# Taps of one block as diagonal matmuls, two vector subtractions fewer, and a new instruction order, in a two-branch sequence kernel

## The chip, the cores and the metric

The kernel runs on one core of a Trainium2 chip. A core has a matrix engine (TensorE, PE in the profile, with its weight loads listed as PEld), a vector engine (VectorE, DVE), an activation engine (ScalarE, ACT), GpSimd (POOL) and SyncE (SP), which here only issues DMAs. The engines run side by side, each through its own instruction list in order, and wait for each other by semaphores. The metric is the device time of one execution in microseconds (us); lower is better.

## The reference

Two independent branches over 2048 positions of 576 channels are computed and set side by side in the output. Branch A is attention with 32 heads of 18 channels, in which each position looks at itself and seven earlier ones, two apart. Branch B gates a long convolution. Its first step, the shift with four taps, is what the change touches.

```python
# A: dilated local attention
q, k, v = split(x @ wqkv)                       # 32 heads of 18
logits  = einsum("bhsd,bhswd->bhsw", q, kg) * scale      # kg: k at s, s-2, ..., s-14
a       = einsum("bhsw,bhswd->bhsd", softmax(logits), vg) @ wo
# B: shift, long convolution, gate
for t in range(4):
    k_shift = k_shift + k_pad[:, t:t + S, :] * shift_k[:, 3 - t]
kv = k_shift * v
y  = irfft(rfft(kv, 2S) * rfft(ssm_k, 2S))[:S] + kv * ssm_D
b  = q * y
out = concatenate([a, b], axis=-1)
```

## The kernel before, in words

**Order.** All work is cut into named jobs, and the string `ORDER` lists the names. The last loop of the kernel calls them in that order, and each engine gets its instructions in the order of the calls; nothing reorders them afterwards. A setup of fixed order goes ahead of the list: loads of x, weights, k and v, index tables and masks on POOL, the tables of sines, the first projections. A quotation mark behind a projection's or output's name means that its short tail matmuls go first instead of last. PSUM is handed out in four slots of two banks each (`banks`, `slots`): a job that finds none free waits for the engine that empties the oldest.

**Branch A.** `q`, `k`, `v` jobs (`project`, line 317) multiply 128x128 weight blocks by 512 columns of x, with tails of 64 rows, and a fifth column tile of 64. `L` jobs (line 701) are the products of queries with shifted keys on DVE; `G` jobs (line 712) sum them over a head's channels on PE with 32 weight columns. `sm` jobs are the softmax, `D` jobs spread its weights by DMA on SP's queue, `V` jobs (line 808) multiply by the values on DVE, `A` jobs (line 816) sum over the eight positions on PE with 64x64 identities, `O` jobs (line 871) are the output projection.

**Branch B.** The sequence is cut into four blocks of 512 positions. `Lk`, `Lv` load a block of k and v. `T0` to `T3` (`taps`, line 511) do the four taps and the product with v. For this k lies seven rows deep in each partition (`kj`), so that a shift is another row; DVE multiplies two rows at a time by the spread taps `skb`, adds the halves into a pair of buffers, and multiplies by v. The result is `kv`. `M` jobs (line 538) fold a block into sums and differences of its two halves, with the matrix `fold` as weights, since position pairs lie in neighbouring partitions. `x` jobs (line 677) transform it to frequencies. `Lf` jobs load the filter by transposing DMAs on SP's queue, `Fr` corrects first rows (six small DMAs on SP's queue, one on POOL's), `F` jobs (line 592) fold the filter and `K` jobs (line 612) transform it. `Lw` loads the weights of v, and `RG` jobs regroup them on ACT. 

For each output block j, third t of the channels and earlier block i, `p` jobs (line 948) multiply spectra on DVE and `z` jobs (line 960) add the products up in PSUM with 64x64 identities on PE. Block 3 takes four products per third. For the thirds named in `JOINED` (line 42), a `y` job (line 957) first subtracts the third product from the first on DVE, and the `z` job of the third product falls away. `i`, `b` and `g` jobs transform back, mirror and multiply by the gate; the stores go out from there.

**Memory.** `Ks` holds 12 parts of 2304 columns. The setup uses the middle and the end for x and for tables; the first parts stay empty until the transformed filters of blocks 3 and 2 are written there by K jobs. `xw` holds x, its weights and the four blocks of kv (`KVS`).

Of the kernel before, what the change touches and what calls it, by code (L numbers as in the profile page):

```python
# [12 lines left out]
ALU = mybir.AluOpType  # L13
FP32 = mybir.dt.float32
BF16 = mybir.dt.bfloat16
# [2 lines left out]
PSUM = bass.MemoryType.PSUM  # L18

ORDER = """  # L20
    T0 k03a' T1 S1 k03b I1 k02a k02b Lk2 Lv2 I0 k00a' Lk3 Lv3 M01 X5 k00b q10a Ex q10b Lf3 T2 Lo3 q13a' q13b
    k10a k10b T3 k13a' Lf2 k13b q12a q12b N2 Lo2 k01a M10 k01b Lf1 M00 k11a k11b q11a M11 q11b Lf0 N3 Lw SV L001
    k12a M20 k12b x001 M21 x021 q24a x020 q24b x000 Lo1 k24a Fr Lo0 Z2 N1 RG3 k24b RG2 F3 RG0 F2 L000 K310 G000
    K311 K210 K211 L002 K313 G001 RG4 F1 G002 L003 G003 K302 L004 G004 K301 L010 K212 L011 K303 K213 K203 N0 F0
    L012 K200 K300 G010 L013 K201 K312 K202 RG1 G011 G012 K113 K103 G013 L014 G014 K112 K102 K101 L100 K100 K010
    K111 K110 sm0a K001 K013 sm0b v24a' L101 v24b L102 G100 L103 G101 K012 sm0c sm0d U3 U2 K000 K011 K003 G102
    K002 D0 D1 v11a v11b G103 L104 G104 ak00 M30 v12a' v12b ak02 v01a ak01 L110 G110 M31 L111 G111 v01b v00a'
    L112 G112 L113 Wl v00b G113 x031 U1 L114 G114 V04 v10a' v10b A04 sm1a sm1b v02a v02b v03a' sm1c v03b x201
    V10 V11 sm1d V12 A10 v13a' v13b D2 x330 x310 x301 V13 A11 V20 V21 x200 x331 x230 x010 x221 A20 x321 V22 x210
    x011 V23 D3 V34 ax02 x220 x030 x300 D4 A21 V40 V41 A34 D5 O000' x211 V42 x320 x231 x111 x131 Tx2 A40 V43  # L30
    x120 x101 ax00 x130 ax01 V50 x121 x311 O001 A41 V51 O100' p000 x100 x110 O010 A50 V52 z000 O011' V53 O101
    A51 Tk2 p010 z010 ax10 O020' O021 p020 z020 O110' ak10 i000 p200 i02880 Q0 p100 z100 p101 p110 p111 Q1 z101
    i02881 i001 p121 p120 O111 z110 p201 z111 z120 p210 z121 O120 p211 z200 z210 z211 p212 z212 z201 p202 z202
    Tx3 p220 Tk3 p221 O030' p222 O121 b0288 z220 p301 z221 O031' p302 b00 z222 p303 i200 i100 g0 Q2 p300 y300
    p312 i12880 i201 i101 i12881 z300 z301 z303 p310 p311 y310 O130 b10 b1288 p313 g1 Q3 p322 O131' z310 p320
    z311 p321 z313 i22880 i300 b20 y320 p323 i22881 i301 b2288 g2 z320 z321 z323 b30 i3384L g30 g3384
"""

LHOMES = (0, 1, 2, 0, 1, 2, 0, 1, 2, 0, 1, 2, 0, 1, 0, 1, 0, 1, 0, 1)
VHOMES = (0, 1, 2, 0, 1, 2, 0, 1, 2, 0, 1, 2, 0, 1, 2, 0, 1, 2)  # L40
OHOMES = (0, 1, 1, 0, 2, 0, 1, 0)
JOINED = ("300 310 320").split()
PHOMES = (0, 1, 2, 3, 0, 1, 2, 3, 0, 4, 1, 2, 3, 0, 4, 1, 2, 3, 0, 1, 2, 3, 0, 1, 2, 3, 0, 1, 2, 3)


def view(t, offset, dims):

    return bass.AP(tensor=t.tensor, offset=t.offset + offset, ap=[list(t.ap[0])] + [list(d) for d in dims])
# [3 lines left out]
def kernel(  # L52
# [13 lines left out]
    nc = tc.nc  # L66
    Bsz, S, D = A_x.shape
# [6 lines left out]
    kf = B_k.flatten_outer_dims()  # L74
    vf = B_v.flatten_outer_dims()
# [45 lines left out]
    def kv_of(i):  # L121
        return view(xw, HB * KVS[i], [[D, 4], [1, D]])
# [26 lines left out]
    tB = sp1.tile([128, 8 * D], BF16, name="tB")  # L149
    skrow = tB[0:97, 0:4 * D]  # L150
    nc.scalar.dma_start(skrow[96:97, :], B_shift_k.rearrange("d j -> (d j)").unsqueeze(0))
    warm = main.tile([128, 1], FP32, name="warm")
    nc.scalar.activation(warm[:], pib[:], ACT.Sin)
    ones96 = sp1.tile([97, 256], BF16, name="ones96")
# [19 lines left out]

    def kTok(m):
        return view(Ks, k_at(m, 2), [[D, 4], [1, D]])
    kjs, vts = [], []
# [6 lines left out]
    def load_k(i):  # L184

        eng = nc.sync
        kj = sp1.tile([128, 7, D], BF16, name="kj", bufs=2)
        r0 = BL * i
        low = [(0, 64)]
        if i == 0:  # L190
            nc.gpsimd.memset(kj[0:1, 0:3, :], 0.0)
            nc.gpsimd.dma_start(kj[0:1, 3:7, :], kf[0:4, :].unsqueeze(0))
            low = [(1, 49), (49, 64)]
        for a, b in ((3, 7), (0, 3)) if i == 0 else ((0, 7),):
            for p0, p1 in low:
# [5 lines left out]
        kjs.append(kj)  # L201

    def load_v(i):
        vt = sp1.tile([128, 4, D], BF16, name="vt", bufs=2)
        nc.sync.dma_start(vt[0:128:2], vf[BL * i:BL * i + 256, :].rearrange("(p c) d -> p c d", c=4))
        nc.sync.dma_start(vt[1:128:2], bass.AP(tensor=vf.tensor, offset=vf.offset + (BL * i + 256 + 3) * D,
                                              ap=[[4 * D, 64], [-D, 4], [1, D]]))
        vts.append(vt)

    def load_filter(m):  # L210

# [49 lines left out]
    for h in range(2):  # L261
        f = fold[:, 64 * h:64 * h + 64]
        nc.gpsimd.affine_select(f, ones128[:, 0:64], pattern=[[-2, 64]], compare_op=ALU.is_equal, fill=0.0,
                                base=0, channel_multiplier=1)
        nc.gpsimd.affine_select(f, f, pattern=[[2, 64]], compare_op=ALU.not_equal, fill=(1.0, -1.0)[h],
                                base=-127, channel_multiplier=1)
    flip2 = main.tile([128, 128], BF16, name="flip2")
    nc.gpsimd.tensor_scalar(flip2[:], flip[:], 2.0, None, op0=ALU.mult)
    ident2 = main.tile([128, 128], BF16, name="ident2")
# [215 lines left out]
    for n in range(2):  # L485
        project_first(1, 2 * n)
        sines[3 - 3 * n]()
    def job(name, fn, *args):

        assert name not in jobs  # L490
        jobs[name] = partial(fn, *args)
# [19 lines left out]
    def taps(i):  # L511
# [23 lines left out]
            add(pair[1])  # L535
        tt(kv, kv, vt, ALU.mult)
# [599 lines left out]
```

## Time and profile before

| | |
|---|---|
| median of 3 runs | 206.83 us (206.75 to 206.92) |
| profiled execution, first to last instruction | 204.6 us |
| instructions | 5004, of them 2074 matmuls |
| largest group on PE, projections of L322 | 38.5 us, 160 matmuls |
| pair products on DVE (L706) | 31.7 us, 16 instructions |
| spectral products on DVE (L950) | 9.5 + 18.9 + 9.5 + 2.7 us by place of the result |
| tap multiplications on DVE (L517) | 19.3 us, 8 instructions |
| evictions of filter units on ACT (L618) | 18.6 us, 32 instructions |
| moved by DMA | 38.48 MB, mean 188 GB/s |

The profiled execution's own time isn't listed apart from its span. The median of the three runs is 2.2 us longer than the span, which leaves out what lies ahead of the first instruction and behind the last.

How to read the profile: a row of a group gives line, engine, operation, tile written and tiles read, shapes and count, then busy time and mean duration, then the idle time of the engine just before it and what ended that. The chain that ended last is followed back from the last instruction, at each step to what released it or to the instruction before it on its engine. A piece of the chain has a start, a length and a count. Matmuls are pipelined, so the duration of one (380 ns for 512 columns) is longer than the distance from one to the next, and a share of busy time alone doesn't prove that PE is full.

### The profile page before, as it was taken

How to read it: one execution, taken by the hardware profiler on the slowest of the kernel's cores; microseconds unless marked ns; L12 is line 12 of the kernel's file. 1: busy time of each engine (PE TensorE's matmuls, PEld its weight loads, DVE VectorE, ACT ScalarE, POOL GpSimd, SP SyncE). 2: the span in 40 equal slices, each digit the busy share in tenths (PEclk: the TensorE clock that was granted, in tenths of full speed). 3: DMA queues.
4: the chain of work that ended last, by engine and by line, in shares of the span. 5: the costliest groups of instructions: out<-in, count | busy, mean ns of one | idle time of the engine just before them, and what ended most of it. 6: DMA issues, size and time to landing. Idle time of an engine off the chain costs nothing.

```text
span 204.6 us, 5004 instructions
## 1 busy us (share of the span) xinstructions
PE 196.9 (96%) x2074; PEld 109.9 (54%) x2074; DVE 192.3 (94%) x146; ACT 155.6 (76%) x223; POOL 60.8 (30%) x106
## 2 busy tenths in 40 slices
PE   7999999999989999999999999999999999999990
PEld 2543544334455646543245556776666767766660
DVE  7559999999999999999999999999999999899992
ACT  4788995678899999966578678886778767767760
POOL 8989500011348581400380000004090001030300
PEclk9999999999999999999999999999999999999997
DMA  6999899989509869999899990879989303944555
GB/s 197 280 293 306 175 289 373 214 177 281 169 3 146 111 82 185 167 180 222 157 235 216 248 244 34 141 183 334 186 227 233 100 28 122 227 130 145 153 182 150
DMA packets 34916, 38.48 MB, mean 188 GB/s; under 512 B 17523, under 2 KB 28911, under 8 KB 34894
## 3 DMA queue, kind: packets, MB, share of 16 engines
q1 hardware_dynamic: 26668, 24.29, 46.5%
q0 software_dynamic: 5760, 11.36, 29.5%
q10 hardware_dynamic: 2466, 2.51, 3.6%
q8 instruction: 16, 0.26, 0.5%
q14 instruction: 6, 0.05, 0.1%
HBM read 13.11 MB, written 4.72 MB: 87 GB/s over the span
## 4 chain that ended last, share of the span: by engine, by line
PE 88%; DMA 3%; ACT 2%; DVE 2%; issue 1%; SPq 1%; DVEq 0%
PE ps_proj L322 18%; PE ps_fx L682 8%; PE ps_wo L888 8%; PE ps_z L975 8%; PE ps_inv L1010 7%; PE ps_acc L824 7%; PE ps_fk L567 5%; PE ps_log L720 5%; DMA Ks<-in_A_x_dram 3%; PE ps_proj L333 3%; PE ps_proj L326 3%; PE ps_proj L439 3%; PE ps_fk L568 3%; PE ps_fold L545 2%; PE ps_wo L880 1%
## 5 line engine op out<-in xcount | busy, mean ns | idle before, releaser
L322 PE MATMUL ps_proj<-xw 128*128 128x512 bf16 x160 | 38.5, 380 | 0.0
L706 DVE TENSOR_TENSOR av<-qk 128x4096 bf16<-128x4096 bf16 (+1 forms) x16 | 31.7, 2014 | 0.1
L322 PEld LDWEIGHTS <-xw 128*128 128x128 bf16 x160 | 13.9, 98 | 19.4 <-issue 5.7
L988 ACT ACTIVATE av<-ps_z 128x768 bf16<-128x768 f32 x23 | 17.2, 811 | 6.5 <-PE ps_z L975 6.0
L517 DVE TENSOR_TENSOR tB<-kj,skb 128x4608 bf16<-128x4608 bf16 (+1 forms) x8 | 19.3, 2416 | 0.1
L950 DVE TENSOR_TENSOR qk<-xw,Ks 128x2304 bf16<-128x2304 bf16 x14 | 18.9, 1354 | 0.3 <-PE ps_z L975 0.3
L684 ACT ACTIVATE xw<-ps_fx 128x576 bf16<-128x576 f32 x32 | 18.6, 665 | 0.3 <-PE ps_fx L682 0.2
L618 ACT ACTIVATE Ks<-ps_fk 128x576 bf16<-128x576 f32 x32 | 18.6, 699 | 0.2 <-PE ps_fk L568 0.2
L355 ACT ACTIVATE qk<-ps_proj 128x1024 bf16<-128x1024 f32 x14 | 14.3, 1023 | 5.2 <-PE ps_proj L333 2.8
L888 PE MATMUL ps_wo<-qk 128*128 128x288 bf16 x128 | 17.9, 287 | 0.0
L626 POOL DMA_DIRECT2D Ks<-Ks x8 | 10.1, 1426 | 26.0 <-PE ps_back L1059 19.3
L682 PE MATMUL ps_fx<-xw,TB 128*128 128x288 bf16 x128 | 17.7, 287 | 0.0
L567 PE MATMUL ps_fk<-Ks,TB 128*128 128x384 bf16 x62 | 16.5, 327 | 0.1
L824 PE MATMUL ps_acc<-av,ident 64*64 64x512 bf16 x160 | 15.3, 378 | 0.0
L1010 PE MATMUL ps_inv<-av,TI 128*128 128x288 bf16 (+1 forms) x112 | 15.2, 292 | 0.0
L568 PE MATMUL ps_fk<-Ks,TB 128*128 128x192 bf16 x62 | 15.2, 246 | 0.0
L682 PEld LDWEIGHTS <-TB 128*128 128x128 bf16 x128 | 11.9, 98 | 5.9 <-issue 2.7
L888 PEld LDWEIGHTS <-qk 128*128 128x128 bf16 x128 | 11.7, 98 | 5.4 <-issue 2.7
L355 ACT ACTIVATE v<-ps_proj 128x1024 bf16<-128x1024 f32 x9 | 9.3, 1033 | 6.5 <-PE ps_proj L322 4.5
L813 DVE TENSOR_TENSOR av<-Ks,v 128x4096 bf16<-128x4096 bf16 x6 | 13.5, 2286 | 0.0
L827 ACT ACTIVATE qk<-ps_acc 128x1024 bf16<-128x1024 f32 x8 | 8.2, 1024 | 6.7 <-PE ps_acc L824 6.7
L1010 PEld LDWEIGHTS <-TI 128*128 128x128 bf16 x112 | 10.6, 98 | 4.2 <-issue 1.1
(195 smaller groups left out, 441.6 us busy)
## 6 DMA issues: line engine op xcount, KB each, us to landing
Ks<-Ks POOLq DMA_DIRECT2D x8, 576.0 KB, 7.8
TB<-av SPq DMA_DIRECT2D x12, 256.0 KB, 5.4
kj<-in_B_k_dram SPq DMA_DIRECT2D x6, 504.0 KB, 7.0
vt<-in_B_v_dram SPq DMA_DIRECT2D x8, 288.0 KB, 5.3
Ks<-av SPq DMA_DIRECT2D x8, 256.0 KB, 5.6
out_dram<-qk ACTq DMA_DIRECT2D x5, 288.0 KB, 3.7
Ks<-in_A_x_dram SPq DMA_DIRECT2D x2, 576.0 KB, 5.4
xw<-in_A_wqkv_dram SPq DMA_DIRECT2D x2, 576.0 KB, 6.2
```

Of the source, the lines that this page charges most:

```text
L322: nc.tensor.matmul(ps[:, jp, :], wq(kb, comp, 128 * ct, 128), xT(kb, 1024 * jj + 512 * jp, 512), **se)
L355: nc.scalar.activation(view(t, o + pad + 1024 * jj, [[512, 2], [1, 512]]), ps[:], ACT.Copy)
L517: tt(to, view(kj, row * D, [[D, n], [D, 4], [1, D]]), view(skb, row * D, [[D, n], [0, 4], [1, D]]), ALU.mult)
L567: nc.tensor.matmul(o[:, 0:2], w, rhs[:, 0:2], start=start, stop=stop)
L568: nc.tensor.matmul(o[:, 2], w, rhs[:, 2], start=start, stop=stop)
L618: nc.scalar.activation(view(Ks, k_at(m, cs ^ (m & 1)) + 96 * gi, [[768, 3], [384, 2], [1, 96]]), acc3(ps), ACT.Copy, scale=(PSG, MSG)[cs][ ...
L682: nc.tensor.matmul(ps[:, pm, 0:HD], TX[:, 2 * pm + c, 128 * gi:128 * gi + 128], kv[:, 2 * c + pm, HD * h:HD * h + HD], start=(c == 0), sto ...
L706: tt(view(P, at, [[step, 4], [256, nj], [1, 256]]), view(t, o + 256 * hh, [[0, 4], [512, nj], [1, 256]]), view(tk, ok + 2 + 8 * ug + 256 * ...
L824: nc.tensor.matmul(acc[64 * o:64 * o + 64, h, :], ident[64 * h:64 * h + 64, 64 * h:64 * h + 64], view(P[s], 256 * u, [[2048, 2], [1, 256]] ...
L888: nc.tensor.matmul(ps[:, r, 0:HD], oT(hh, j + 2 * r, t)[:, o:o + 128], wo[:, t // 2, t % 2, HD * h:HD * h + HD], start=(t == 0 and not fli ...
L950: tt(product_home(n), view(xw, HB * XG[i] + QTR * t, [[HB, 3], [1, QTR]]), view(Ks, k_at(j - i, 0) + QTR * t, [[HB, 3], [1, QTR]]), ALU.mult)
L1010: nc.tensor.matmul(ps[:, c, 0:n], TI[:, sl, pm, 128 * c:128 * c + 128], Yall(j % 2, pm, sl, slice(c0, c0 + n)), start=(pm == 0 and sl == 0 ...
```

## The change

Four things change.

1. **Block 3's taps go to PE.** k of block 3 is loaded by two transposing DMAs, channels in partitions, into the empty start of `Ks`. For each of the four taps a diagonal matrix of tap weights is built once on DVE in the setup (`diag`, `diag_t`, from `taps_w`, which two more loads on ACT's queue bring). A matmul with shifted columns of k as weights (every fourth position, a stride of four elements) and a diagonal as the moving operand gives shifted k times tap; four taps add up in PSUM. `T30`, `T31` do 64 such matmuls each with 128 moving columns, `T3t` does 32 with 64. DVE then multiplies PSUM by v, which is loaded straight into the place of kv, and the result is written over it.
2. **Another fold for block 3**, since its positions now lie in two halves of the partitions: `fold_t`, two small additions on POOL.
3. **`JOINED` keeps only 310.** `y300` and `y320` go, `z302` and `z322` come.
4. **`ORDER` is another string.** Every engine's sequence changes with it. The list before stands in the kernel above; the new one is in the diff.

```diff
 ORDER = """
+    k03a' T0 Lk2 S1 k01a k02a k01b k03b Lf1 Lv2 Lf2 Lo2 k02b q12a M01 T1 k00a' k00b Lf0 X5 k11a k11b q13a' T2 I1
+    q13b N2 q10a k10a Lf3 k10b q10b Lw k24a q11a q11b Lk3 k12a Fr q12b Lo3 k12b Lv3 k24b M00 q24a q24b F2 M20
+    k13a' K211 SV k13b L000 RG0 G000 L002 Lo1 K212 N3 L001 F3 G001 N1 N0 G002 K210 L003 L004 RG4 K213 RG1 RG3
+    L010 Z2 G003 Lo0 F1 G004 L011 T30 RG2 T31 K200 T3t K201 K311 K203 K313 L012 K300 G010 K302 L013 F0 G011 K202
+    K303 G012 L014 K310 G013 L100 G014 K101 K301 K102 K013 K011 K312 sm0a sm0b v24a' v02a K100 G100 v02b L101
+    L102 v24b L103 sm0c sm0d G101 G102 L104 K001 K010 K110 K113 G103 K012 L110 K112 K000 G104 K002 L111 K111
+    v00a' v00b D1 G110 L112 U3 K103 K003 G111 x020 x031 v01a v01b G112 M21 L113 L114 G113 I0 v03a' G114 v03b
+    v10a' V11 M30 x231 v10b V10 sm1a x220 A10 v13a' sm1b Wl D0 D2 V04 v13b V13 x010 A04 sm1c v11a V12 x030 v11b
+    M10 A11 U2 M31 v12a' v12b sm1d D3 V20 x021 x000 x301 x011 V21 ak00 A20 V22 x300 V23 x230 x001 D4 x210 ax00
+    x201 A21 x200 O000' ak01 M11 V34 D5 x211 A34 ax02 x310 ak02 x221 O100' O101 Tx2 x111 ax01 x100 V40 V41 A40
+    U1 x120 O001 V42 V43 x101 Tk2 V50 x130 x320 A41 V51 x131 x311 V52 x121 x331 x321 A50 x110 O010 p000 z000
+    x330 O011' V53 A51 p010 z010 O110' ax10 p020 O111 z020 p101 O020' O021 Q1 ak10 p100 p110 i02880 z100 z101
+    i000 p120 i02881 p121 z120 p111 p200 z121 i001 p210 p211 z110 z111 O120 z200 b00 p212 p201 z210 z211 p202 Q0
+    z212 Tx3 z201 p220 i12880 z202 p221 p222 b0288 i12881 i100 z220 z221 p301 p302 z222 Tk3 g0 Q2 i101 i200
+    b1288 b10 i22880 p303 O030' O031' p300 i22881 z300 z302 g1 z301 z303 O130 p310 i201 O121 b20 p312 y310 b2288
+    p311 z310 z311 p313 p320 p322 z313 p323 O131' i300 p321 z320 Ex z322 Q3 i301 z321 g2 z323 b30 i3384L g30
+    g3384
 """
-JOINED = ("300 310 320").split()
+JOINED = ("310").split()
...
+    taps_w = main.tile([128, 5, 4], BF16, name="taps_w")
+    nc.scalar.dma_start(taps_w[:, 0:4, :], B_shift_k[0:512, :].rearrange("(kb p) j -> p kb j", p=128))
+    nc.scalar.dma_start(taps_w[64:128, 4, :], B_shift_k[512:576, :])
...
+    TURNED = (3,)
+    KT = 16 + BL
+    diag = view(Ks, 3 * HB, [[512, 4], [128, 4], [1, 128]])
+    diag_t = view(Ks, 3 * HB + 2048, [[64, 4], [1, 64]])[64:128]
...
+        if i in TURNED:
+            t = view(Ks, 0, [[1, 5 * KT]]) if i == TURNED[0] else sp1.tile([128, 7, D], BF16, name="kj", bufs=2)
+            rows = kf[BL * i - 16:BL * i + BL]
+            eng.dma_start_transpose(view(t, 0, [[KT, 4], [1, KT]]), rows[:, 0:512])
+            eng.dma_start_transpose(view(t, 4 * KT, [[1, KT]]), rows[:, 448:576])
+            kjs[i] = t
+            return
...
+        if i in TURNED:
+            nc.sync.dma_start(kv_of(i)[0:64], vf[BL * i:BL * i + 256, :].rearrange("(p c) d -> p c d", c=4))
+            nc.sync.dma_start(kv_of(i)[64:128], bass.AP(tensor=vf.tensor, offset=vf.offset + (BL * i + 256 + 3) * D,
+                                                        ap=[[4 * D, 64], [-D, 4], [1, D]]))
+            return
...
+    fold_t = main.tile([128, 128], BF16, name="fold_t")
+    for h in range(2):
+        nc.gpsimd.tensor_tensor(fold_t[:, 64 * h:64 * h + 64], ident[:, 0:64], flip[:, 0:64], (ALU.add, ALU.subtract)[h])
...
+    nc.vector.tensor_tensor(diag, ident[:].unsqueeze(1).unsqueeze(1).to_broadcast([128, 4, 4, 128]),
+                            taps_w[:, 0:4, :].unsqueeze(3).to_broadcast([128, 4, 4, 128]), ALU.mult)
+    nc.vector.tensor_tensor(diag_t, ident[64:128, 64:128].unsqueeze(1).to_broadcast([64, 4, 64]),
+                            taps_w[64:128, 4, :].unsqueeze(2).to_broadcast([64, 4, 64]), ALU.mult)
...
+    def turned(i, kb, c, j, e):
+        return view(kjs[i], KT * kb + 16 + (259 - c if e else c) - j, [[4, 64]])
+
+    def taps_pe(i, h):
+        ps, slot = banks("ps_tap")
+        for c in range(2):
+            for kb in range(4):
+                for j in (3, 2, 1, 0):
+                    for e in range(2):
+                        nc.tensor.matmul(ps[64 * e:64 * e + 64, c, 128 * kb:128 * kb + 128],
+                                         turned(i, kb, 2 * h + c, j, e), diag[:, kb, j, :],
+                                         start=(j == 3), stop=(j == 0), tile_position=(0, 64 * e))
+        kv = kv_of(i)[:, 2 * h:2 * h + 2, 0:512]
+        tt(kv, ps[:], kv, ALU.mult)
+        slots.append(slot)
+
+    def taps_pe_tail(i):
+        ps, slot = banks("ps_tap")
+        for c in range(4):
+            for j in (3, 2, 1, 0):
+                for e in range(2):
+                    nc.tensor.matmul(ps[64 * e:64 * e + 64, 0, 64 * c:64 * c + 64], turned(i, 4, c, j, e)[64:128],
+                                     diag_t[:, j, :], start=(j == 3), stop=(j == 0), tile_position=(64, 64 * e))
+        kv = kv_of(i)[:, :, 512:576]
+        tt(kv, view(ps, 0, [[64, 4], [1, 64]]), kv, ALU.mult)
+        slots.append(slot)
...
-                    nc.tensor.matmul(pss[pm][64 * e:64 * e + 64, h, 0:HD], fold[:, 64 * pm:64 * pm + 64],
+                    nc.tensor.matmul(pss[pm][64 * e:64 * e + 64, h, 0:HD], (fold_t if i in TURNED else fold)[:, 64 * pm:64 * pm + 64],
...
-        job(f"T{i}", taps, i)
+        if i in TURNED:
+            for h in range(2):
+                job(f"T{i}{h}", taps_pe, i, h)
+            job(f"T{i}t", taps_pe_tail, i)
+        else:
+            job(f"T{i}", taps, i)
```

More of the change, by code (lines that the diff above doesn't have):

```diff
@@ L20 @@
 ORDER = """
[L21 to L35, printed above, removed]
@@ L36 @@
-    z311 p321 z313 i22880 i300 b20 y320 p323 i22881 i301 b2288 g2 z320 z321 z323 b30 i3384L g30 g3384
+    k03a' T0 Lk2 S1 k01a k02a k01b k03b Lf1 Lv2 Lf2 Lo2 k02b q12a M01 T1 k00a' k00b Lf0 X5 k11a k11b q13a' T2 I1
+    q13b N2 q10a k10a Lf3 k10b q10b Lw k24a q11a q11b Lk3 k12a Fr q12b Lo3 k12b Lv3 k24b M00 q24a q24b F2 M20
+    k13a' K211 SV k13b L000 RG0 G000 L002 Lo1 K212 N3 L001 F3 G001 N1 N0 G002 K210 L003 L004 RG4 K213 RG1 RG3
+    L010 Z2 G003 Lo0 F1 G004 L011 T30 RG2 T31 K200 T3t K201 K311 K203 K313 L012 K300 G010 K302 L013 F0 G011 K202
@@ L176, in kTok @@
         return view(Ks, k_at(m, 2), [[D, 4], [1, D]])
-    kjs, vts = [], []
+    kjs, vts = {}, {}
+    TURNED = (3,)
+    KT = 16 + BL
+    diag = view(Ks, 3 * HB, [[512, 4], [128, 4], [1, 128]])
+    diag_t = view(Ks, 3 * HB + 2048, [[64, 4], [1, 64]])[64:128]
     def load_x(qtr):
@@ L200, in load_k @@
                                                     ap=[[4 * D, 64], [-D, b - a], [1, D]]))
-        kjs.append(kj)
+        kjs[i] = kj
     def load_v(i):
+        if i in TURNED:
[3 more added lines that the diff above has]
+            return
         vt = sp1.tile([128, 4, D], BF16, name="vt", bufs=2)
@@ L207, in load_v @@
                                               ap=[[4 * D, 64], [-D, 4], [1, D]]))
-        vts.append(vt)
+        vts[i] = vt
     def load_filter(m):
```

## Prediction

> **What bounds the kernel now.** First the page: busy shares, then the shares of the chain that ended last.
>
> ```profile
> PE 196.9 (96%) x2074; PEld 109.9 (54%) x2074; DVE 192.3 (94%) x146; ACT 155.6 (76%) x223; POOL 60.8 (30%) x106
> ...
> PE 88%; DMA 3%; ACT 2%; DVE 2%; issue 1%; SPq 1%; DVEq 0%
> ```
>
> Two engines look full, TensorE (PE) and VectorE (DVE). The chain runs over PE for 88% of the span, over DVE for 2%. Next the waits: who stood still for whom (total, times, longest).
>
> ```profile
> PEld L720 <- DVE av L706: 0.9, 1, 0.9
> ...
> PE ps_log L720 <- DVE av L706: 0.6, 1, 0.6
> ...
> DVE xw L517 <- DMA kj<-in_B_k_dram: 4.2, 1, 4.2
> ```
>
> The longest wait of PE for DVE is under 1 us. DVE's one long wait is 4.2 us for the first k block, at the start. So neither engine idles; the question is whether PE's busy time is real work. The chain in order of time answers it (start, length, piece, matmuls):
>
> ```profile
> 18.59 1.83 PE ps_proj L322 x8
> 20.42 0.57 PE ps_ti L397 x16
> ...
> 24.04 0.97 PE ps_proj L322 x4
> ...
> 29.10 3.56 PE ps_proj L322 x16
> ...
> 121.15 1.85 PE ps_acc L824 x32
> ...
> 143.36 1.73 PE ps_acc L824 x32
> 145.08 0.65 PE ps_z L975 x16
> ...
> 181.92 2.07 PE ps_z L975 x48
> ```
>
> From 8 to 16 matmuls of 512 columns the projection takes 1.73 us more: 0.216 us each. From 4 to 8 it is 0.86 us, the same 0.215. Taking 0.216 each off the 0.97 of the piece of four leaves 0.11 us. That rest is a fixed cost at a **change of tile shape**: the piece at 143.36 is followed by matmuls of its own shape (64x64), the equal piece at 121.15 by 128x128 ones, and it takes 0.12 us more. Matmuls thus stream at one unvarying rate and pay about 0.12 us whenever the shape changes. PE is the bound from about 10 to 197 us; DVE runs beside it, nearly as full.
>
> The Trainium skill (Perfetto Trace Analysis, Identifying the Most-Contended Engine) says that matmul busy time is a poor measure of a full TensorE and that the busy share of weight loads should be used. By that rule 54% would leave PE room and DVE would be the bound. The constant spacing above disagrees with it for this kernel; what it would give is the first rival.
>
> **The change part by part.** *Taps of block 3 leave DVE.* The DVE timeline of T3:
>
> ```profile
> 44.36 2.55 DVE L517 TENSOR_TENSOR tB<-kj,skb 128x4608 bf16<-128x4608 bf16 x1
> 46.94 1.36 DVE L520 TENSOR_TENSOR xw<-tB 128x2304 bf16<-128x2304 bf16 x1
> 48.34 2.56 DVE L517 TENSOR_TENSOR tB<-kj,skb 128x4608 bf16<-128x4608 bf16 x1
> 50.93 2.75 DVE L520 TENSOR_TENSOR xw<-xw,tB 128x2304 bf16<-128x2304 bf16 x2
> 53.71 1.36 DVE L536 TENSOR_TENSOR xw<-xw,vt 128x2304 bf16<-128x2304 bf16 x1
> 54.99 0.51 DVE L590 TENSOR_SCALAR Ks<-Ks 1x576 bf16<-1x576 bf16 x2
> ```
>
> That is 54.99 - 44.36 = 10.6 us gone. In its place come three products that read float32 PSUM: 128x1024 twice, 128x256 once. The groups by form have the kin:
>
> ```profile
> L1020 DVE TENSOR_TENSOR TB<-ps_back,TB 128x384 bf16<-128x384 f32 x2 | 1.0, 554 | 0.6 <-PE ps_back L1038 0.6
> L1020 DVE TENSOR_TENSOR TB<-ps_back,TB 128x768 bf16<-128x768 f32 x1 | 1.0, 954 | 0.0
> L748 DVE TENSOR_TENSOR av<-av 128x2048 bf16<-128x2048 bf16 x1 | 1.2, 1225 | 0.0
> ```
>
> 400 ns for 384 elements: 1.04 ns each and 154 ns fixed, so 1.22 + 1.22 + 0.42 = 2.9 us. DVE also builds the diagonals: 2048 elements cost between 1.2 us (L748's row) and 2.3 us (at 1.04 ns each); the small one at most 0.4. I take 2.7 us, hidden in DVE's 4.2 us wait for the first k block; uncovered it would push T0, and DVE has that much given back later.
>
> *Two of three subtractions go*: L958 runs in one engine slot, from
>
> ```profile
> 193.24 1.35 DVE L958 TENSOR_TENSOR av<-av,qk 128x2304 bf16<-128x2304 bf16 x1
> 194.50 1.35 DVE L950 TENSOR_TENSOR qk<-xw,Ks 128x2304 bf16<-128x2304 bf16 x1
> ```
>
> 1.26 us each, so 2.5 us. DVE in all: -10.6 + 2.9 - 2.5 = -10.2 us behind the start. DVE is not the end of the chain, so this buys only the places where PE waits for it.
>
> *What PE gains.* T30 and T31: 2 x 64 matmuls, 64 weight columns and 128 moving columns, in pairs on two column halves. That is exactly the form of L397: 0.57 us for 16, less 0.12 for the shape change, 28 ns each; 128 x 28 ns = 3.6 us. The weights here are read with a stride of four, which no row shows. If loads hide no better than not at all, the row of the loads gives the other end:
>
> ```profile
> L397 PEld LDWEIGHTS <-TB 128*64 128x64 bf16 x32 | 1.0, 109 | 0.7 <-issue 0.7
> ```
>
> 160 x 109 ns = 17.4 us for T3 whole. I take L397's spacing, the nearest row. T3t: 32 matmuls of 64 columns, between half of L397's rate and the same, 0.45 to 0.9 us; I take 0.9, since the loads are as many. The sums z302 and z322 return, 16 matmuls each: 0.65 us each (the piece at 145.08; a third of 2.07 gives 0.69), 1.3 us.
>
> *The new order.* The two order strings can be walked job by job: whole projections, K, F, x, i, smc are 128x128; their tails 64x128; the fifth column tile, M, X5, I, T30 and T31 128x64; G 128x32; A, z, b, T3t and the tails of the fifth tile and of O 64x64. Before, that makes 54 + 24 + 16 + 15 + 14 = 123 runs of one shape (128x128, 64x64, 64x128, 128x32, 128x64), 122 changes; after, 68 + 37 + 19 + 17 + 16 = 157 runs, 156 changes. Most of the 34 more lie behind A10, where attention sums, x units and output projections are now cut finer. 34 x 0.12 = 4.1 us, all on the bound engine.
>
> *Start.* Two more small loads sit on ACT's queue ahead of its first work, and many tiny packets beside the first x load. Nothing shows their cost but L151's issue:
>
> ```profile
> 0.83 0.52 ACTq L151 DMA_DIRECT2D tB<-in_B_shift_k_dram  x1
> ```
>
> Between 0 and 1.0 us; I take 0.3, since ACT also waits for PE there. POOL's two small additions for fold_t lie in its setup, long before M30.
>
> *What comes back.* Off PE the chain has two long stretches, before the first filter units and in the products:
>
> ```profile
> 56.93 0.67 ACT xw L780
> ...
> 58.12 1.16 ACT Ks L605 x2
> 59.28 1.16 ACT xw L780
> 60.44 0.54 ACT Ks L605
> ...
> 163.54 0.69 DVE qk L950
> ...
> 164.82 1.35 DVE av L950
> 166.17 1.37 DVE Ks L950
> ```
>
> 4.1 and 4.0 us. PE was not idle through them:
>
> ```profile
> 50.00:60.00 10.00, 9.65 (x79) 5.05 (x76) 9.79 (x9) 9.07 (x13) 2.61 (x6) 1.00 0.43 124
> ...
> 160.00:170.00 10.00, 9.83 (x193) 6.87 (x191) 9.45 (x8) 6.65 (x11) 0.00 (x0) 1.00 0.16 54
> ```
>
> (columns: span, PE, PEld, DVE, ACT, POOL, granted clock, DMA, GB/s). The clock is full. PE lacks 0.35 and 0.17 us there, at most 4 us if matmul ends are modelled long. A DVE 10 us ahead ends the second stretch; F2 and F3 now stand apart, which eases the first. I take 2.5 us back and 1.3 us of new waits: 1.2 net, bounds 4 back and 5 lost.
>
> **Sum** on the profiled span: 3.6 + 0.9 + 1.3 + 4.1 + 0.3 - 1.2 = +9.0 us, 204.6 to 213.6. The median of the runs, 206.83, lies 2.2 us above the span; with that, **215.8 us**.
>
> **Rivals.** *DVE was the bound.* Then the 10.2 us come off: 196.6. For it: 94% busy, and the stretch at 163.54. Against it: that stretch is 4 us out of 204.6, and the spacing of matmuls. It decides if PE can take in 10 us more without moving its last matmul, which needs idle time that the windows don't show. 4 in 100; another 2 that it all cancels to within 0.2%.
>
> *Weight loads of T3 lie open.* The strided loads fail to hide: 17.4 us in place of 4.5, 228.7. Against it L397, whose 16 matmuls with their loads took 0.57 us, where 16 open loads alone would be 1.7. From half open (222) on it would be seen. 7 in 100. The Trainium skill (TensorE: Matmul & The Clock Gate, The mechanism) says that weight loads overlap running matmuls only where row groups differ, and T30's two halves share theirs; by its load figure (columns over 1.2, 53 ns) 160 open loads would be an estimate of 8.5 us, 219.8 in all. L397's halves share their rows too, and the trace disagrees.
>
> *T30 waits for its inputs.* Lk3 and Lv3 stand on SP's queue behind four filter transposes, Lw and, for Lv3, the six row moves of Fr:
>
> ```profile
> 22.32 1.97 SPq L237 DMA_TRANSPOSE xw<-in_A_x_dram  x1
> ...
> 27.68 0.63 SPq L206 DMA_DIRECT2D vt<-in_B_v_dram  x1
> ...
> 35.02 14.07 SPq L213 DMA_TRANSPOSE Ks<-in_B_ssm_k_dram  x4
> ...
> 51.02 8.74 SPq L582 DMA_DIRECT2D Ks<-Ks  x6
> ```
>
> ```profile
> vt<-in_B_v_dram SPq DMA_DIRECT2D x8, 288.0 KB, 5.3
> ```
>
> From 27 us: Lv2 1.3, transposes 7.9 to 14.1, Lw 1.7, Lk3 4 to 7, Fr 8.7: Lv3 is issued between 51 and 60, landing 5.3 us later (median in the row of the DMA issues). Added up at the rates above from 18.6 us, where the first listed job has its body, the PE jobs ahead of T30 reach about 59 us. If v lands at 65, DVE stands at T30's product with L012 and all later pair products behind it, two of four PSUM slots are held, and PE waits for G012: 4 us, 220. 15 in 100.
>
> *The new order wins back more*, 4 us: 213 or somewhat under. Speaks for it: DVE far ahead. 14 in 100.
>
> **Numbers.** Forecast (213 to 218.5) 58 in 100; more won back (209 to 213) 14; late inputs (218.5 to 221.5) 15; open loads 7; DVE bound 4; no change 2. A difference under 0.2% can't be told from none here. Range 211.5 to 221, which leaves out the open loads, the faster cases and the far edge of the win: some 18 in 100. Slower 0.94, same 0.02, faster 0.04.
>
> **What would show it.** Right: DVE busy falls to about 185 us, PE stays dense and its last matmul comes some 9 us later; T30's 64 matmuls take about 1.8 us; shape changes still cost 0.12 us; DVE now waits for PE. Wrong: T30 at 7 us (open loads); DVE waiting for vt or kj near 60 us (late inputs); a PE that ends earlier although it does more, which would make its busy time a sham.

## The result and the profile after

The changed kernel took 232.86 us in the median of four runs (230.8 to 237.4), the kernel before 206.88 us on the same chip: 1.1172 times as long, 95% interval 1.114 to 1.1204, or 231.1 us at 206.88. Two of the four runs, and one to three runs of five later kernels, took longer and are left out of the ratios, so kernels are compared by ratio below, or by their medians where no run is left out. The forecast was 215.8, the range ended at 221. The direction was right; 15.3 us of the 24.2 were not foreseen.

The page of the changed kernel (span 229.4 us), busy shares and then the chain that ended last:

```profile
PE 211.2 (92%) x2255; PEld 116.8 (51%) x2266; DVE 186.2 (81%) x143; ACT 163.7 (71%) x228; POOL 78.8 (34%) x108
...
PE 75%; ACT 10%; DMA 8%; issue 3%; DVE 2%; DVEq 0%; ACTq 0%
```

DVE fell from 192.3 to 186.2 us; about 185 had been worked out. PE's busy time rose by 14.3 us, the span by 24.8. The chain, 88% PE before, is 75% PE, and ACT and DMA hold 18% of it. So PE now stands still, and the waits say for whom (who, for whom: total, times, longest):

```profile
DVE v L766 <- ACT v L378: 4.9, 1, 4.9
ACT TB L954 <- DMA out_dram<-TB: 4.7, 1, 4.7
...
PE ps_z L1035 <- ACT TB L954: 3.5, 1, 3.5
...
ACT qk L954 <- DMA out_dram<-qk: 2.9, 1, 2.9
...
DVE xw L579 <- DMA xw<-in_B_v_dram: 2.5, 1, 2.5
```

Before, no wait of PE past the start was longer than 0.6 us. The stretches of the changed kernel (span, PE, PEld, DVE, ACT, POOL, granted clock, DMA share, GB/s) show where and what it cost in clock:

```profile
80.00:90.00 10.00, 6.61 (x55) 2.66 (x54) 5.31 (x3) 8.93 (x9) 2.45 (x2) 0.92 0.64 118
90.00:100.00 10.00, 9.84 (x64) 4.89 (x62) 8.14 (x5) 6.34 (x10) 0.00 (x0) 0.74 0.54 107
...
170.00:180.00 10.00, 6.51 (x64) 3.93 (x62) 4.85 (x5) 4.40 (x8) 1.24 (x1) 0.86 0.85 216
```

PE lost 3.4 us between 80 and 90 and 3.5 between 170 and 180, where before no window from 20 to 200 lay under 9.4. Behind the first of these holes the granted clock is 0.74: PE counts as busy for 9.84 us there, but at a lower clock, so the busy time overstates the added work. Narrower stretches show that the clock there is either full or half:

```profile
84.99:88.40 3.41, 0.90 (x11) 0.31 (x10) 3.41 (x2) 3.36 (x4) 0.00 (x0) 1.00 0.94 173
88.40:91.81 3.41, 2.58 (x15) 1.17 (x15) 3.41 (x3) 1.00 (x3) 0.00 (x0) 0.50 0.02 5
...
173.74:177.15 3.41, 0.88 (x24) 0.71 (x23) 0.31 (x1) 1.19 (x2) 0.93 (x1) 1.00 0.74 154
177.15:180.56 3.41, 3.41 (x21) 1.96 (x14) 3.41 (x3) 2.71 (x4) 0.00 (x0) 0.50 0.64 153
```

It is half for 6.8 us from 88.4 on and for 3.4 us from 177.2 on, and full elsewhere between the first microseconds and the end of PE's work. Three places are read more closely.

**The hole at 80 us.** ACT's timeline (start, length, line, operation) of the changed kernel:

```profile
76.62 3.36 ACT L678 ACTIVATE Ks<-ps_fk 128x576 bf16<-128x576 f32 x6
80.00 1.28 ACT L812 ACT_TABLE_LOAD   x1
81.29 1.91 ACT L812 ACTIVATE av<-av 128x2048 bf16<-128x2048 bf16 x1
...
83.64 1.93 ACT L378 ACTIVATE v<-ps_proj 128x1024 bf16<-128x1024 f32 x2
85.58 1.28 ACT L823 ACT_TABLE_LOAD   x1
...
87.28 1.28 ACT L824 ACT_TABLE_LOAD   x1
```

Two things meet. `Ex`, which loads the function table that serves both exponential and logarithm, stood ahead of the softmax before (at 28 us). In the new order it stands near the end (at 218 us), behind all softmax work, so exponential and logarithm change tables against each other: five loads of 1.28 us (three here, two at 121.6 and 123.2). And `L101`, the next pair product on DVE, stands behind `v02b`, whose eviction (L378) waits on ACT behind seven filter evictions, the first table load and an exponential. DVE waits 4.9 us, and the sums on PE wait for DVE.

**The hole at 170 us.** The chain in order of time in the changed kernel:

```profile
163.94 11.55 DMA out_dram<-TB
...
175.57 0.66 ACT TB L954
...
176.27 1.33 PE ps_z L1035 x24
```

`O020` evicts into the staging buffer (`OHOMES`, line 42) from which `O011` has just been stored, and has to wait for the landing: 11.55 us. The copy holds ACT, `z` evictions queue behind it, and PE runs out of slots. At 204.03 it happens again with another buffer (`O130` behind `O031`, landing 7.08 us).

**T30's inputs.** SP's timeline and DVE's in the changed kernel:

```profile
50.80 7.05 SPq L642 DMA_DIRECT2D Ks<-Ks  x6
...
58.55 0.68 SPq L221 DMA_DIRECT2D xw<-in_B_v_dram  x1
```

```profile
65.06 2.36 DVE L579 TENSOR_TENSOR xw<-ps_tap,xw 128x1024 bf16<-128x1024 f32 x2 [2.46 <-DMA xw<-in_B_v_dram]
67.33 0.41 DVE L590 TENSOR_TENSOR xw<-ps_tap,xw 128x256 bf16<-128x256 f32 x1
```

v is issued behind the six row moves of `Fr` and T30's product starts at 65 us, as that rival had it. DVE loses 2.5 us there, PE almost nothing. The products take 2.36 and 0.41 us, as worked out (2.9).

### The profile page after: what moved, and what is told of

Read it like the earlier page. It is cut to its first block, busy times and chain, and to the rows that moved or that the text cites. A ratio compares the mean times of both kernels' runs of the same rounds, so it can differ in the third digit from the quotient of the medians.

```text
span 229.4 us, 5385 instructions
## 1 busy us (share of the span) xinstructions
PE 211.2 (92%) x2255; PEld 116.8 (51%) x2266; DVE 186.2 (81%) x143; ACT 163.7 (71%) x228; POOL 78.8 (34%) x108
## 4 chain that ended last, share of the span: by engine, by line
PE 75%; ACT 10%; DMA 8%; issue 3%; DVE 2%; DVEq 0%; ACTq 0%
PE ps_proj L345 13%; PE ps_fx L742 7%; PE ps_z L1035 6%; PE ps_inv L1070 6%; PE ps_acc L884 6%; PE ps_fk L627 5%; DMA out_dram<-TB 5%; PE ps_log L780 4%; PE ps_wo L948 4%; PE ps_proj L462 3%; DMA out_dram<-qk 3%; PE ps_fk L628 2%; PE ps_proj L356 2%; PE ps_rev L662 2%; PE ps_fold L600 2%
## 5 line engine op out<-in xcount | busy, mean ns | idle before, releaser
L345 PE MATMUL ps_proj<-xw 128*128 128x512 bf16 x150 | 37.3, 380 | 1.2 <-issue 1.0
L678 ACT ACTIVATE Ks<-ps_fk 128x576 bf16<-128x576 f32 x32 | 19.3, 657 | 7.6 <-PE ps_fk L628 7.5
L345 PEld LDWEIGHTS <-xw 128*128 128x128 bf16 x160 | 14.0, 98 | 18.6 <-issue 5.2
L1048 ACT ACTIVATE av<-ps_z 128x768 bf16<-128x768 f32 x23 | 17.4, 809 | 6.0 <-PE ps_z L1035 5.4
L378 ACT ACTIVATE qk<-ps_proj 128x1024 bf16<-128x1024 f32 x14 | 14.3, 1025 | 10.1 <-PE ps_proj L356 8.0
L744 ACT ACTIVATE xw<-ps_fx 128x576 bf16<-128x576 f32 x32 | 19.1, 658 | 1.4 <-PE ps_fx L742 1.4
L742 PE MATMUL ps_fx<-xw,TB 128*128 128x288 bf16 x128 | 18.4, 287 | 0.0
L627 PE MATMUL ps_fk<-Ks,TB 128*128 128x384 bf16 x62 | 18.1, 351 | 0.0
L686 POOL DMA_DIRECT2D xw<-xw x2 | 2.4, 1212 | 45.3 <-ACT qk L887 38.4
L1070 PE MATMUL ps_inv<-av,TI 128*128 128x288 bf16 (+1 forms) x112 | 17.7, 310 | 0.0
L884 PE MATMUL ps_acc<-av,ident 64*64 64x512 bf16 x160 | 15.3, 379 | 1.1 <-ACT xw L744 1.1
L628 PE MATMUL ps_fk<-Ks,TB 128*128 128x192 bf16 x62 | 16.1, 260 | 0.0
L545 DVE TENSOR_TENSOR tB<-kj,skb 128x4608 bf16<-128x4608 bf16 (+1 forms) x6 | 14.3, 2382 | 0.1
L766 DVE TENSOR_TENSOR v<-qk 128x4096 bf16<-128x4096 bf16 x4 | 9.2, 2289 | 5.4 <-ACT v L378 4.9
```

What stands on the lines that cost most here:

```text
L345: nc.tensor.matmul(ps[:, jp, :], wq(kb, comp, 128 * ct, 128), xT(kb, 1024 * jj + 512 * jp, 512), **se)
L627: nc.tensor.matmul(o[:, 0:2], w, rhs[:, 0:2], start=start, stop=stop)
L628: nc.tensor.matmul(o[:, 2], w, rhs[:, 2], start=start, stop=stop)
L678: nc.scalar.activation(view(Ks, k_at(m, cs ^ (m & 1)) + 96 * gi, [[768, 3], [384, 2], [1, 96]]), acc3(ps), ACT.Copy, scale=(PSG, MSG)[cs][ ...
L742: nc.tensor.matmul(ps[:, pm, 0:HD], TX[:, 2 * pm + c, 128 * gi:128 * gi + 128], kv[:, 2 * c + pm, HD * h:HD * h + HD], start=(c == 0), sto ...
L744: nc.scalar.activation(view(xw, HB * XG[i] + 96 * gi + 1152 * h, [[HB, 2], [384, 3], [1, 96]]), view(ps, 0, [[512, 2], [96, 3], [1, 96]]), ...
```

## The experiments

Two explanations stood for the 15 us: the **work** added to PE is dearer than summed (taps, shape changes, sums), or the new order's **waits** are. The first three runs measure work in the old order, the fourth the order alone, the next four take the named waits out of the changed kernel, and the others follow what came up then. Diffs of `ORDER` show only the stretch that differs.

### Work alone, in the order before

**Taps of block 3 on PE, nothing else moved.** The kernel before with the new tap code of the change, all three thirds joined:

```diff
-k10a k10b T3 k13a'
+k10a k10b k13a'
-q11b Lf0 N3 Lw
+q11b T30 Lf0 T31 N3 T3t Lw
```

> The kernel before with one part of the change: the taps of block 3 on TensorE (T30, T31, T3t placed where T3's DVE work began to be free, behind q11b), all three subtractions kept, the order otherwise that of before; 124 shape changes against 122. Theory A (TensorE is the bound, the taps cost what their matmuls take, 5 to 6 us in the changed kernel's trace, less what PE waited for VectorE): 210 to 213 us. Rival 1 (the taps bring more than their matmuls, by weight loads or slots held): 216 us or more. Rival 2 (VectorE was the bound): below 205 us.

212.74 us against 206.70, +6.0 us (ratio 1.0303, 1.0266 to 1.034). Its groups by line:

```profile
L574 PE MATMUL ps_tap<-Ks 128*64 128x128 bf16 x128 | 4.2, 226 | 0.0
...
L586 PE MATMUL ps_tap<-Ks 64*64 64x64 bf16 x32 | 1.2, 224 | 0.0
```

33 ns per matmul in place of 28, so 4.2 us in place of 3.6; 1.2 in place of 0.9. These are busy times, to the end of the last matmul. From start to start, as the 28 were read, it is 31 ns: 4.11 us from the first tap to the first of `T3t`, less one shape change, for 128. The first body that stands at 18.59 in the kernel before stands half a microsecond later in this one's chain:

```profile
19.12 1.83 PE ps_proj L344 x8
```

4.2 + 1.2 + 0.5 and two shape changes (0.2) make 6.1 of the 6.0 measured. The work itself is about 1 us dearer than summed, not 15. With stride-four weights the loads still hide: 160 of them open at 109 ns would be 17.4 us.

**Two joins taken back, nothing else:**

```diff
-JOINED = ("300 310 320").split()
+JOINED = ("310").split()
-p300 y300 p312
+p300 p312
-z300 z301
+z300 z302 z301
-b20 y320 p323
+b20 p323
-z320 z321
+z320 z322 z321
```

> The kernel before with only the two subtractions y300 and y320 taken out and z302 and z322 put in. Theory A (TensorE is the bound): 32 matmuls more, 1.3 us, time 207.5 to 208.5 us. Rival (VectorE is the bound in the products): 2.5 us less, 204 to 205.5 us.

207.93 against 206.70: +1.2 us (1.0066, 1.0038 to 1.0094). The term of 1.3 holds.

**More shape changes, nothing else.** Every quotation mark in the order before is dropped, so that tails stand behind their bodies: 144 changes of tile shape in place of 122, the same work.

```diff
-T0 k03a' T1 S1 k03b
+T0 k03a T1 S1 k03b
```

> The kernel before with every quotation mark taken out of its order: the same jobs in the same order with the same matmuls, but the tails of all projections and outputs stand last, and so the tile shape changes 144 times instead of 122. If a change of shape costs 0.12 us on the bound engine: 22 x 0.12 = 2.6 us more, 209 to 210 us. Rival (the matmuls in flight hide it, or the stages are bound elsewhere): 206.5 to 207.5 us.

209.07 against 206.75: +2.3 us (1.0121, 1.0086 to 1.0155), some 0.106 us for each of the 22. The unit price of 0.12, read from two pieces of the chain, was right within the interval (0.08 to 0.15).

### The order alone

The kernel before, taps on DVE, with the new order: T3 right behind `Lv3`, all three joins kept, 153 shape changes. Against the new string (the lines with the joins are left out):

```diff
-k12b Lv3 k24b
+k12b Lv3 T3 k24b
-G004 L011 T30 RG2 T31 K200 T3t K201
+G004 L011 RG2 K200 K201
```

> The kernel before with the new order alone: T3 stays on VectorE (placed behind Lv3, ahead of the first pair product) and all three subtractions stay; 153 shape changes against 122. Theory A (the parts on TensorE cost 7.3 us, as run alone; the rest of the 24 us is the order's, 3.7 us by shape changes and the other by waits): 219 to 225 us. Rival (the order is only bad together with the taps on TensorE): 210 to 214 us.

242.02 us, ratio 1.1709 (1.1674 to 1.1744): neither number. The order alone is slower than the whole change. Waits of this run, PE's and then DVE's, and its windows:

```profile
PE ps_log L721 <- DVE av L707: 14.8, 3, 12.7
```

```profile
DVE tB L518 <- DMA kj<-in_B_k_dram: 8.2, 1, 8.2
```

```profile
50.00:60.00 10.00, 2.94 (x20) 1.16 (x14) 7.43 (x4) 4.35 (x6) 3.64 (x4) 0.79 0.69 157
60.00:70.00 10.00, 4.34 (x24) 2.23 (x24) 9.80 (x7) 0.95 (x2) 0.00 (x0) 0.53 0.09 32
```

T3 waits 8.2 us for k of block 3, then takes DVE for 10.7 us (52.5 to 63.2) ahead of the pair products for which PE waits. So the parts don't add up: with T3 on DVE at this place the new order costs more than with the taps on PE. Another place for T3 was not tried, so the price of the order alone isn't settled. But most of its other waits are there too (4.4 us for the staging buffer, 5.0 for v), without any new tap code.

### The waits taken out one by one

**The table early.** The changed kernel with `Ex` ahead of the softmax again:

```diff
-T1 k00a' k00b Lf0
+T1 k00a' Ex k00b Lf0
-p321 z320 Ex z322
+p321 z320 z322
```

> The changed kernel with one job moved: Ex, which loads ScalarE's exponential table ahead of use, goes from the end of the order to just ahead of k00b. In the changed kernel's trace five more table loads of 1.28 us stand inside the two softmax steps. Theory A (the loads hold up ScalarE's evictions there, and TensorE waits for those): the loads at the softmax lines are gone, the idle stretches of PE near 80-90 and 117-125 us shrink, time 222 to 226 us. Rival (the stretch near 80 us is L101 standing behind the eviction of v02b and a backlog of filter evictions, and the loads merely lie inside it): 229 to 231 us.

Ratio 1.1072 (1.1007 to 1.1138): 1.0 point less than the change, 2.1 us. The five loads are gone (6.4 us of ACT), but L101's wait is nearly as long (waits of this run):

```profile
DVE v L766 <- ACT v L378: 4.7, 1, 4.7
```

So the rival was nearer: the loads lay in the hole and made it deeper, but the projection makes it. The clock didn't fall behind this hole. Two stretches of this run, as long as the half-clock stretch above:

```profile
86.26:89.68 3.42, 1.88 (x20) 1.04 (x20) 2.53 (x2) 2.54 (x4) 0.00 (x0) 1.00 1.10 204
89.68:93.09 3.41, 1.83 (x23) 0.86 (x16) 3.41 (x2) 0.14 (x1) 0.00 (x0) 1.00 0.31 56
```

PE idles for 3.1 us in all, 1.5 and 1.6 in each, and the clock stays at 1.00; in the changed kernel 2.5 of 3.41 us were idle in one such stretch, and half clock followed. This execution has half clock elsewhere, for 3.4 us each from 69.2 and from 175.0 on.

**The output projections later**, so that the store before has landed:

```diff
-z020 p101 O020' O021 Q1
+z020 p101 Q1
-z110 z111 O120 z200
+z110 z111 O020' O021 z200
-i12880 z202 p221
+i12880 z202 O120 p221
-z301 z303 O130 p310
+z301 z303 p310
-z313 p323 O131'
+z313 p323 O130 O131'
```

> The changed kernel with O020, O021, O120 and O130 moved later in the order, so that the store that frees their staging buffer has had time to land. Nothing else is moved. Theory B (ScalarE stands at the output copy until the earlier store from the same buffer has landed, 11.6 us after its issue, and TensorE stands behind it): the waits of the output copy for out_dram are gone, PE no longer idles near 172-176 and 209-211 us, time 224 to 227 us. Rival (the stores are late because the DMA queues are crowded there, so that gate loads or sums wait in place of the copies): 229 to 231 us.

1.0934 (1.0877 to 1.0991): 2.4 points less, 4.9 us. The windows of this run:

```profile
160.00:170.00 10.00, 8.77 (x127) 5.18 (x126) 9.88 (x8) 7.99 (x13) 3.89 (x6) 1.00 1.07 248
170.00:180.00 10.00, 9.86 (x143) 6.51 (x142) 9.35 (x8) 7.82 (x13) 1.24 (x1) 1.00 0.75 175
```

and the landing times of its stores, from the view of the output's tile:

```profile
DMA to landing us min/median/max: 1.7/2.4/11.4
```

The slowest store takes as long as before, 11.4 us, but ACT no longer waits for it, PE has 18.6 busy us in 20 in place of 16.5, and the clock stays full.

**L101 ahead of the v projections:**

```diff
-v24a' v02a K100 G100 v02b L101
+v24a' L101 v02a K100 G100 v02b
```

> The changed kernel with one job moved: L101 ahead of v02a in place of behind v02b, so that it no longer stands behind the eviction of v02b (in the changed kernel's trace VectorE waits 4.9 us there, until ScalarE has worked off six filter evictions, a table load and the exponential). Theory C (that place makes TensorE idle near 80-90 us and its granted clock drop behind it): the wait is gone, 223 to 227 us. Rival (the stretch is bound by ScalarE's backlog before the softmax sums, whatever VectorE does): 229 to 231 us.

1.1032 (1.0967 to 1.1097): 1.4 points less, 2.9 us, between the two. The wait for v is gone, but one for the filter's first rows at `N1` is 4.5 us, where the changed kernel had 1.7 (waits of this run):

```profile
DVE Ks L650 <- DMA Ks<-Ks: 4.5, 1, 4.5
```

`N1` stands ahead of `L101` in the order, so the move can't have made this wait: these rows land earlier or later from execution to execution.

**All three:**

> The changed kernel with all three moves together: Ex early, O020, O021, O120 and O130 later, L101 ahead of v02a. Alone the first gave about 2 us and the second about 4.6. Theory (the excess over 215.8 us is made of these waits, and they add): 215 to 219 us, PE busy near 100% in all stretches of 20 us. Rival (waits only move on to the next tight place): 222 us or more.

1.0622 (1.0589 to 1.0654): 5.5 points less, 11.4 us, a little over the sum of the three (9.9) and, by the intervals, not different from it. That is three quarters of what wasn't foreseen. The longest wait of PE in its profiled execution (223.0 us) is one for the small moves of `Fr`:

```profile
PE ps_rev L662 <- DMA Ks<-Ks: 2.4, 1, 2.4
```

### SP's queue, where waits change places

From here on each kernel contains the three edits.

**Rows later**: `N1`, `N0` and `F1` moved behind the work that doesn't need `Fr`.

```diff
-F3 G001 N1 N0 G002
+F3 G001 G002
-G003 Lo0 F1 G004 L011 T30 RG2 T31 K200
+G003 Lo0 G004 L011 N1 T30 RG2 T31 F1 K200
-L013 F0
+L013 N0 F0
```

> The kernel with all three moves (219.4 us in its undisturbed runs) and a fourth: N1, N0 and F1, which need the row moves of Fr, stand behind L011 and the taps in place of ahead of them; 154 shape changes. In the trace of the kernel with three moves VectorE stands 3.8 us at N1 and PE 2.4 us at F1 for these DMAs. Theory (what is left above 215.8 us is this wait): gone from both engines, 214.5 to 217.5 us. Rival (T30 then stands for its own inputs, or the next filter units for F1): 218 to 221 us.

223.34 us in the median, 218.6 at the least; they scatter too far for a ratio, and no gain can be told. PE's and DVE's longest waits in the profiled execution, which took 224.65 us:

```profile
PE ps_fk L627 <- DVE xw L579: 4.1, 1, 4.1
```

```profile
DVE xw L579 <- DMA xw<-in_B_v_dram: 4.6, 1, 4.6
```

In this execution that is the rival of late inputs as it was priced: DVE stands at T30's product until v lands at 67.4 us, and PE loses 4.1 us. Whether the execution of 218.6 us had this wait isn't known. In the changed kernel DVE had other waits ahead of this product, which fits that PE lost next to nothing there.

**Nine fewer shape changes** in that kernel, by the quotation marks of k24a, q11a, v00a, v03a, O000, O011 and O030, set where they were missing and taken away where they stood (145 in place of 154); two of them:

```diff
-q10b Lw k24a q11a q11b
+q10b Lw k24a' q11a' q11b
-v00a' v00b D1
+v00a v00b D1
```

> The kernel with four moves, and seven projections and outputs with their tails at the other end, so that the shape changes 145 times instead of 154. By the price of 0.106 us that the order of before without its marks gave (2.3 us for 22): 1.0 us less than the kernel with four moves. Rival (the tails moved ahead wait for something): no less.

1.0596 (1.0547 to 1.0645); 217.6 to 224.2 us. The least times of the two kernels differ by 1.0 us, about the forecast for nine changes, but the scatter is 6 us: not shown.

**v ahead of k on SP's queue**, so that it no longer stands behind `Fr`:

```diff
-q11b Lk3 k12a Fr q12b Lo3 k12b Lv3 k24b
+q11b Lv3 Lk3 k12a Fr q12b Lo3 k12b k24b
```

> The kernel with four moves and a fifth: Lv3 ahead of Lk3 on SP's queue instead of behind the row moves of Fr; 154 shape changes. In the trace of the kernel with four moves v of block 3 was issued at 60.8 us and landed at 67.4, VectorE stood 4.6 us at T30's product and PE 4.1 us behind it. Theory (the last large wait that the new order brought is this one): gone, 214 to 217 us, and the runs lie closer together. Rival (Fr, now later, holds up F1 and the filter units in its place): 218 to 222 us.

1.062 (1.0569 to 1.0671). The wait for v is gone and the next one is there; the chain of the profiled execution, which took 223.17 us:

```profile
55.47 6.36 DMA Ks<-Ks
...
61.84 3.31 DMA Ks<-Ks
...
65.17 1.56 DMA Ks<-Ks
...
66.87 1.14 PE ps_rev L662 x8
```

Now three of the dependent moves of `Fr` take 11.3 us and end at 66.7, and `F1` waits for them with `T3t` behind it on PE.

**F1 behind K313** as well:

```diff
-L011 N1 T30 RG2 T31 F1 K200 T3t K201 K311 K203 K313 L012
+L011 T30 RG2 T31 K200 T3t K201 K311 K203 K313 N1 F1 L012
```

> The kernel with five moves, and N1 and F1 moved once more, behind the units of filters 2 and 3 (K313), so that the row moves of Fr have some 9 us more to land. Theory (PE's 3.3 us at F1 were the last large wait of the new order between 50 and 80 us; without it the time is that of PE's work): 214.5 to 217 us. Rival (something else in that stretch, such as the filter units' evictions, then holds PE up): 218 us or more.

1.0574 (1.0544 to 1.0604), 218.87 us, and the six runs lie within 1.3 us. The least times of the four kernels from all three edits to this one are 219.4, 218.6, 218.1 and 218.1: the queue's edits hardly moved the best execution. The waits above were read in executions of 223.0 to 224.7 us, and none over 219.4 is left here. With six executions, and an interval that overlaps that of all three edits, a gain by these last edits is likely but not shown. In those three profiles the clock is half for 3.4, 6.8 and 3.4 us between 63 and 75 us; in this one it is full from 6.4 us to the end of PE's work. The page of this run, then PE's longest waits:

```profile
span 217.2 us, 5375 instructions
...
PE 206.2 (95%) x2255; PEld 114.4 (53%) x2266; DVE 186.0 (86%) x143; ACT 157.6 (73%) x223; POOL 79.3 (36%) x108
```

```profile
PE ps_inv L1070 <- ACT av L1048: 1.4, 1, 1.4
...
PE ps_fk L627 <- DMA Ks<-Ks: 0.8, 1, 0.8
...
PE ps_z L1035 <- ACT v L1125: 0.6, 1, 0.6
PE ps_z L1035 <- DVE qk L1010: 0.4, 1, 0.4
```

The long waits are gone; PE is 95% busy, and 11.9 us over the kernel before remain. PE does the same 2255 matmuls as in the changed kernel in 5.0 us less busy time (211.2 - 206.2) and with 7.2 us less idle time (18.2 - 11.0): so the 12.2 us between the two spans are some 7 of waiting and some 5 of slower work. That agrees with the clock: 10.2 us at half clock in the changed kernel (6.8 + 3.4), none here, are 5.1 us of work at full clock. The 11.9 can be added up from the runs above: taps with their start and two shape changes 6.0, sums 1.2, the 30 other shape changes at 0.106 us 3.2, together 10.4. The 1.5 us left are less than the 3.2 us of waits just shown; that these make them isn't shown.

### Does the kernel before gain by fewer shape changes?

The quotation marks of k01a, k11a and k12a turned round, 118 changes in place of 122:

```diff
-k01a M10 k01b Lf1 M00 k11a k11b
+k01a' M10 k01b Lf1 M00 k11a' k11b
-k12a M20 k12b
+k12a' M20 k12b
```

> The kernel before with the tails of three key projections (k01, k11, k12) first, so that the shape changes 118 times instead of 122. By 0.106 us for a change: 0.4 us faster than before, 206.2 to 206.5 us. Rival (no difference that can be told, since VectorE is as full in that stretch): 206.6 to 206.9 us.

206.19 us (12 runs) against 206.47 (17): 0.9996 (0.9979 to 1.0014). The expected 0.4 us would be 0.998, at the edge of the interval; no difference is shown. No kernel tried here is faster than the one before beyond that.

## Why the prediction was right and where it failed

- **PE as the bound: right.** Less work on DVE bought nothing in the two runs that took it away in the old order. DVE's idle time grew from 12 to 43 us while the kernel got slower, and the added PE work alone, in the old order, costs its own length (+6.0 and +1.2 us). The rivals "DVE was bound" and "open loads" are out, by the ratio 1.0303 and by 31 to 33 ns a matmul.
- **The unit of a shape change, 0.12 us: right** (0.106 by the run with 22 more). The trace of the changed kernel has the 34 more that were counted.
- **The taps: right in kind, about 1 us small.** 31 ns a matmul from start to start, 33 by busy time, and not 28; T3t 1.2 and not 0.9; the start 0.5 and not 0.3.
- **DVE's share: right.** Products 2.8 us, DVE 186.2 us in all, 1.4 over the sum.
- **Late inputs (15 in 100): the mechanism was there, the price in another kernel.** In the changed kernel it cost DVE 2.5 us and PE next to nothing; with the waits ahead of it gone, PE lost 4.1 us to it in one execution (224.65 us), and 4 had been worked out; that they agree so closely is luck, as the landings vary.
- **"I take 2.5 us back and 1.3 of new waits: 1.2 net, bounds 4 back and 5 lost": this step failed.** No run shows anything that came back, and PE had no wait over 0.6 us to give. And new waits cost far more than the bound of 5: 12.4 us of the change's 24.2 go away by moving jobs alone (1.1172 to 1.0574), 11.4 of them by the first three edits, and about 1.5 remain. With 2.7 us here (1.5 in place of -1.2), the taps' 1.0, and 0.8 less for sums and shape changes, the remaining 2.9 us between forecast and the best reordered kernel are accounted for: 11.9 against 9.0.

What lay behind the failed step: the prediction walked the new order for one queue, SP's, and for shape changes. It didn't walk it for ACT. There three things could be read from the strings and the code: `Ex` had gone from ahead of the softmax to the end, `L101` stood behind a projection that is evicted on ACT, and output projections share staging buffers. The fourth could not be read from the order. The distance from `O011` to `O020` is no shorter than before: ACT gets there 6.9 us after the store's issue, where it took 4.1. The store is slower. In the kernel before, ACT's timeline and POOL's:

```profile
148.16 0.38 ACTq L898 DMA_DIRECT2D out_dram<-TB  x1
...
152.25 1.44 ACT L894 ACTIVATE TB<-ps_wo 128x576 bf16<-128x576 f32 x2
```

```profile
148.53 0.75 POOL L932 DMA_DIRECT2D TB<-in_B_q_dram  x1 [6.29 <-DVE qk L813]
```

The buffer was free, at the latest, 4.1 us after its store was issued, and the six loads of q that POOL issues came behind that store. In the changed kernel POOL issues a large row move and the first loads ahead of the store (163.94):

```profile
160.15 1.18 POOL L686 DMA_DIRECT2D Ks<-Ks  x1 [6.11 <-DMA out_dram<-qk]
162.71 0.75 POOL L992 DMA_DIRECT2D TB<-in_B_q_dram  x1 [1.39 <-DVE qk L873]
```

and the DMA share of that window is 1.07. That the store queues behind these transfers fits both traces; it is argued, since no run moved POOL's loads. That the waits for stores cost about 4.9 us is shown by the run that moved the output projections.

The prediction also counted every wait at its own length. A hole costs more where the clock falls behind it: some 5 of the 12.2 us between the two spans are slower work, not standing still. Its "one unvarying rate" of matmuls holds for the kernel before, where the clock is full, and not behind these holes.

## What to carry to other kernels

When an order is changed, walk it for each engine that has its own list, and ask of each job what it evicts, which buffer it writes and which table it needs; a count of work on the bound engine alone gave 10 of 24 us here. A wait hidden behind another is seen only once the first is gone, so repeat the trace after every removal. And a trade of work between engines pays only if the engine that takes it has idle time in the very stretch: 6 us off an engine that nobody waited for bought nothing.

## What the hardware showed that wasn't expected

- **The clock falls to half behind a hole in PE's work, for whole stretches of 3.41 us.** In the changed kernel 2.5 of the 3.41 us ahead of 88.40 and of 177.15 were idle; half clock followed for 6.83 and for 3.41 us. With `Ex` early a hole of 3.1 us lay with 1.5 and 1.6 us in two stretches, and the clock stayed at 1.00. In the order-alone run it was half from 55.8 to 69.5, four such stretches. The 15 traces, cut into steps of 3.41 us from the first full clock on, have 14 such falls ahead of PE's last matmul. Each came behind a step in which PE was idle for 1.66 us or more, and the clock never stayed full behind a step with more than 1.74: about half a step of idle time is enough. The Trainium skill (TensorE: Matmul & The Clock Gate, What's actually happening) says that the gate passes half the pulses after an idle window of about 3.4 us and all of them after an equal busy one; the trace agrees in the two rates and in the length, but the window need not be idle throughout.
- **A change of activation table takes 1.28 us of ACT, and no more here.** The load at 80.00 ended at 81.28, and the next operation starts at 81.29. The Trainium skill (ScalarE: Activation LUTs, What ACT_TABLE_LOAD costs) adds a drain of about 1.38 us to the load; no gap of that size stands in this trace, and it differs.
- **A store's landing varies more than sixfold.** In the run with later outputs the shortest is 1.7 us, the median 2.4, the longest 11.4, and that one lies in a window with a DMA share of 1.07.
- **Three tiny dependent moves (1.1 KB each) took 11.3 us** where they were on the path: 6.4 us for one, 1.6 for another. The four kernels ahead of the last one scattered over 3.6 to 6.6 us from run to run, the last, in which `F1` stands behind them with more room, over 1.3; that the moves make the difference is not shown.
